# A Fourier mixing stage ahead of two expert layers: two bias products side by side on row halves

## Chip, cores and metric

The kernel runs on one core of a Trainium2 chip. The metric is the device time of one execution in microseconds (us), as a median of several runs.

## The reference

```python
def _attn_ref(x, w_r, w_i, b_r, b_i):            # x: 2 x 3008 x 256
    X = np.fft.rfft(x, axis=1)
    Xr, Xi = X.real, X.imag
    Yr = Xr @ w_r - Xi @ w_i + b_r
    Yi = Xr @ w_i + Xi @ w_r + b_i
    Yr = np.sign(Yr) * np.maximum(np.abs(Yr) - 0.01, 0.0)
    Yi = np.sign(Yi) * np.maximum(np.abs(Yi) - 0.01, 0.0)
    return np.fft.irfft(Yr + 1j * Yi, n=3008, axis=1)

h = x @ moe_w_in                                  # 6016 tokens, 256 -> 2048
x = (h * np.clip(h + 3.0, 0.0, 6.0) / 6.0) @ moe_w_out
g = x @ moe2_w_gate                               # 256 -> 1536
out = (g / (1 + np.exp(-g)) * (x @ moe2_w_val)) @ moe2_w_out
```

## The kernel before

All of it is one program on one core, its order written out by hand: each engine gets its instructions in the order in which the Python code issues them. The first stage, to about 160 us, is the Fourier mixing; the two expert layers fill the rest.

**The start.** `prepare` issues the loads of the first batch of x on SyncE's queue (SP), with the mixing weights `lin` among them, then the first table `load_m(0, 0)`; GpSimd loads the bias (`b_st`, 64 rows). Sixteen steps `halves1(i)` (L317) do the first transform; each ends in a copy out of PSUM, on ScalarE for even i and on VectorE for odd i (L321). `amid` hangs small jobs behind some of these copies: at 7 GpSimd makes the sum and the difference of the two weight tables (`mixed`, L279); `shifts` adds the threshold to the bias on VectorE (L290), copies it to float32r on ScalarE (L291) and subtracts for the low part on VectorE (L136); `hi` copies a weight table to float32r on ScalarE (L282) and `lo` subtracts for its low part on VectorE (L136). `s2` (L363) needs all sixteen copies.

**The quads.** There are 12 quads p = 0 to 11 (`ORDER`, two batches of six). For each, `s2` does the second transform (64 rows high, two row halves), `ln(p, h)` for h = 0, 1 the mixing, and `ia` (L443, 64 rows high, two row halves) the first inverse. `ln` takes a PSUM tile p3 of one bank, puts the bias into it with one product of 128 rows and 512 columns (L418: `ones`, which holds ones in rows 0 and 32, times `shift`), adds 12 full-height products of 256 columns (L413 to L415), takes a second bank p4 for six more, copies that out (`k1`, L424, ScalarE) and adds it to p3 on VectorE (`yb`, L426), which ends the use of p3. A usual quad runs ln(p, 0), s2(p + 1), ia(p - 1), ln(p, 1). Around quads 3 and 4 the eight steps `quarters1` (L333, 64x64 products on two banks each) of the second batch lie between; quad 4 begins ln(4, 0), `quarters1(3)`, ia(3), `quarters1(4)`. From quad 8 on (`FROM`), `post` (L556, 48 rows high) and `unit` (full height) lie between.

The eight PSUM banks are handed out in a fixed turn by `any_bank`:

```python
turn[0] = (turn[0] + 1) % 8
return (acc_bank if turn[0] in (2, 5, 7) else bank)(shape, name)
```

With each `ln` one step of the weight conversion (`conv1.step`) is queued on ScalarE and VectorE.

Of the kernel before, what the change touches and what calls it, by code (L numbers as in the profile page):

```python
# [14 lines left out]
ALU = mybir.AluOpType  # L15
# [5 lines left out]
SEQ, DIM, NB = 3008, 256, 2  # L21
N1, NG, NJ, K2 = 47, 24, 32, 64
GC = 2 * NG
NQ = NG // 4
LAM = 0.01
# [56 lines left out]
def fourier_moe_kernel(ctx: ExitStack, tc: tile.TileContext, x, lin, bias, w1, w2, fwd1, inv2, fwd2,  # L82
                       inv1, out):
    nc = tc.nc
# [33 lines left out]
    psf = [any_bank]  # L118
    few = [False]

    def woven(t):

        return t.rearrange("p (a b) -> p b a", a=2)

    def pairwise(t):

        return t.rearrange("p (b a) -> p b a", a=2)
# [7 lines left out]
    def low(o, full, hi):  # L135
        nc.vector.tensor_tensor(out=o, in0=full, in1=hi.bitcast(F32), op=ALU.subtract)  # L136
# [87 lines left out]
    zeros = xs_p.tile([128, 512], F32, tag="r", name="zeros", bufs=3)  # L224
# [4 lines left out]
    shift = ap_.tile([128, 2 * DIM], F32R, name="shift")  # L229
    ones = ap_.tile([128, 128], F32R, name="ones")  # L230
# [5 lines left out]
    def ring4(name):  # L236
        return ap_.tile([128, 4 * DIM], F32, tag="bc", name=name, bufs=2)
# [4 lines left out]
    def load_x(b, k, c=slice(0, RC), every=((0, 1),)):  # L242
        for p, step in every:
            nc.sync.dma_start(room[b, k][p::step, c], x[b, k, p::step, c])
# [9 lines left out]
    p = psf[0]([128, 512], "p0")  # L254
# [4 lines left out]
    def prepare():  # L259
        lin_st = ring4("lin_st").rearrange("p (k a b) -> p k a b", k=2, a=2)  # L260
        b_st = spread("b_st")
        load_x(0, 1, every=some)
        load_x(0, 2, every=some)
        nc.sync.dma_start(lin_st, lin)
        for c in (slice(0, 2 * TC), slice(2 * TC, RC)):
            load_x(0, 3, c, some)
        load_m(0, 0)
        nc.gpsimd.dma_start(b_st[:64], bias)
        o = spread("o_st")[:, :128]
        nc.gpsimd.memset(o, 0.0)  # L270
        for r in (0, 32):
            nc.gpsimd.memset(o[r : r + 1], 1.0)
        nc.gpsimd.tensor_copy(ones, o)
        nc.gpsimd.tensor_copy(shift[64:], zeros[64:])
        w = [lin_st[:, k] for k in range(2)]

        def mixed(op):
            w.append(spread("mixed").rearrange("p (a b) -> p a b", b=DIM))
            nc.gpsimd.tensor_tensor(out=w[-1], in0=w[1], in1=w[0], op=op)  # L279

        def hi(i, k):
            nc.scalar.copy(linh[:, i], w[k])  # L282

        def lo(i, k):
            low(linl[:, i], w[k], linh[:, i])

        def shifts(i):
            b = b_st[:64]
            if i == 0:
                nc.vector.tensor_scalar(b, b, LAM, None, op0=ALU.add)  # L290
                nc.scalar.copy(shift[:64], b)  # L291
            else:
                low(shift[32:64], b[32:], shift[32:64])

        amid.update({
            7: [lambda: mixed(ALU.subtract), lambda: mixed(ALU.add)], 8: [lambda: shifts(0)], 9: [lambda: shifts(1)],
            12: [lambda: hi(2, 0)], 13: [lambda: lo(2, 0)], 14: [lambda: hi(0, 2), lambda: lo(0, 2)],
            15: [lambda: hi(1, 3), lambda: lo(1, 3)]})

    amid = {}  # L300

    def spread(name):
        return xs_p.tile([128, 2 * DIM], F32, tag="r", name=name, bufs=3)
# [41 lines left out]
    def table(tag, src, Q, n, name):  # L345
        t = ap_.tile([128, n, 128], F32, tag=tag, name=name, bufs=2)
        nc.sync.dma_start(t, src[:, Q * n * 128 : (Q + 1) * n * 128].rearrange("r (g c) -> r g c", g=n))
        return t

    def load_m(b, Q):  # L350
        if (b, Q) not in m_t:
            m_t[b, Q] = table("m", fwd2, Q, 8, f"m{b}_{Q}")
# [34 lines left out]
    def flush():  # L387
        while due:
            due.pop(0)()
# [8 lines left out]
    def ln(b, Q, h):  # L398

        if (b, Q) not in n_t:  # L400
            n_t[b, Q] = table("n", inv1, Q, 4, f"n{b}_{Q}")
        if ORDER.index((b, Q)) <= FROM:
            conv1.step()
        flush()
        xs = [t[:, :, :, h * 128 : (h + 1) * 128] for t in X[b, Q]]

        def product(o, form, k, start):
            o = pairwise(o)
            for dh in range(2):
                xh, xl = (t[:, dh, form] for t in xs)  # L410
                wh, wl = linh[:, k, dh], linl[:, k, dh]
                wh, wl = woven(wh), woven(wl)
                nc.tensor.matmul(o, xh, wl, start=start and dh == 0, stop=False, skip_group_check=not start)  # L413
                nc.tensor.matmul(o, xh, wh, start=False, stop=False, skip_group_check=not start)
                nc.tensor.matmul(o, xl, wh, start=False, stop=dh == 1, skip_group_check=not start)  # L415

        p = psf[0]([128, 2, DIM], f"p3_{b}_{Q}_{h}")
        nc.tensor.matmul(pairwise(p.rearrange("r c d -> r (c d)")), ones, woven(shift), start=True, stop=True)  # L418
        product(p[:, 1], 0, 0, False)
        product(p[:, 0], 1, 1, False)  # L420
        p1 = psf[0]([128, DIM], f"p4_{b}_{Q}_{h}")
        product(p1, 2, 2, True)
        k1 = ap_.tile([128, DIM], F32, tag="k1", name=f"k1{b}_{Q}_{h}", bufs=2)
        nc.scalar.copy(k1, p1)  # L424
        yb = xs_p.tile([128, 2, DIM], F32, tag="r", name=f"yb{b}_{Q}_{h}", bufs=3)
        nc.vector.tensor_tensor(out=yb, in0=p, in1=k1.unsqueeze(1).to_broadcast([128, 2, DIM]), op=ALU.add)  # L426
        yc = xs_p.tile([128, 2, DIM], F32, tag="r", name=f"yc{b}_{Q}_{h}", bufs=3)
        y = yp[b, Q, h] = ap_.tile([128, 2, DIM], F32, tag="yp", name=f"yp{b}_{Q}_{h}", bufs=3)

        def then():  # L430
            nc.scalar.activation(yc, yb, AF.Relu, bias=edges)
            nc.vector.scalar_tensor_tensor(out=y, in0=yb, scalar=0.0, in1=yc, op0=ALU.min, op1=ALU.add)

        later.append(then)

    def ia(b, Q):
        c4 = ring4(f"cs{b}_{Q}")
        p = [psf[0]([128, 2, DIM], f"p5_{b}_{Q}_{i}") for i in range(2)]
        for h in range(2):
            for c in range(2):  # L440
                for i in range(2):
                    r = slice(64 * i, 64 * i + 64)
                    nc.tensor.matmul(p[i][:, h], n_t[b, Q][r, 2 * h + c, :], yp[b, Q, h][r, c, :], start=c == 0,  # L443
                                     stop=c == 1, tile_position=(64 * i, 0))
        for i in range(2):
            nc.scalar.copy(c4.rearrange("r (h i d) -> r i h d", i=2, d=DIM)[:, i], p[i])
        nc.gpsimd.dma_start(Cd[b][:, Q * 4 * DIM : (Q + 1) * 4 * DIM], c4)
# [4 lines left out]
    ORDER = [(b, Q) for b in range(NB) for Q in range(NQ)]  # L452
    FROM = 8
# [8 lines left out]
    def L(p):  # L462
        return [lambda h=h: ln(*ORDER[p], h) for h in range(2)]

    def A(p):
        return [lambda: ia(*ORDER[p])] if p >= 0 else []
# [159 lines left out]
    at = [0]  # L626
# [130 lines left out]
    halves = [(z - a) // 2 for a, z in pairs]  # L757
# [404 lines left out]
    for q in range(len(quads2) + 1):  # L1162
        if q < len(quads2) and quads2[q][1] == 0 and quads2[q][0] + 1 < len(pairs):
            p = quads2[q][0] + 1
# [63 lines left out]
```

## Time and profile before

| | us |
|---|---|
| median of 3 runs | 1129.22 |
| lowest, highest | 1127.73, 1958.57 |
| profiled execution | 1128.69 |
| its span on the core | 1126.9 |

The profile is of one execution; it shows, for each engine, its instructions with start and length, what they waited for, and the chain of waits that ended last. A line such as L418 is a line of the kernel. "PE" is TensorE's products, "PEld" its weight loads, DVE VectorE, ACT ScalarE, POOL GpSimd, SP SyncE with its DMA queue. Lengths of products are modelled; the distance between starts is the safer measure.

### The profile page before, as it was taken

The numbers are of one execution on the slowest core, as the hardware profiler recorded it, in microseconds if no ns is written. First come the engines' busy times: TensorE is split into PE (matmuls) and PEld (weight loads), VectorE is DVE, ScalarE is ACT, GpSimd is POOL, SyncE is SP. The second block draws the span as 40 slices with busy tenths as digits, with TensorE's granted clock in tenths as the row PEclk, the third lists the DMA queues.
The fourth block names the chain that finished last, engine by engine and source line by source line (L and its number), as shares of the span: only waits on it lengthen the run. The fifth ranks groups of instructions, "written<-read, shape, count | busy, mean of one in ns | idle before, by whom it ended". The sixth has DMA issues, their size and how long they took to land.

```text
span 1126.9 us, 19804 instructions
## 1 busy us (share of the span) xinstructions
PE 1115.0 (99%) x7468; PEld 989.5 (88%) x7468; DVE 909.5 (81%) x1635; ACT 775.8 (69%) x1440; POOL 43.0 (4%) x68
## 2 busy tenths in 40 slices
PE   8999999999999999999999999999999999999998
PEld 7999888888888888888899888888888888888997
DVE  5888887999999999999988777777777777777765
ACT  4767676788787787877777666666666656666655
POOL 3000006300000000000000000000000000000000
PEclk9999999999999999999999999999999999999999
DMA  7756335864483573644553544644644644644552
GB/s 294 289 189 229 115 118 177 287 220 144 138 278 107 182 254 108 220 172 138 211 202 140 196 165 162 241 161 165 238 163 165 236 168 169 238 168 168 209 207 75
DMA packets 62944, 211.49 MB, mean 188 GB/s; under 512 B 5984, under 2 KB 23552, under 8 KB 51392
## 3 DMA queue, kind: packets, MB, share of 16 engines
q1 hardware_dynamic: 60784, 203.61, 52.1%
q0 software_dynamic: 1776, 6.42, 1.4%
q8 instruction: 59, 0.97, 0.3%
q14 instruction: 37, 0.30, 0.1%
q10 hardware_dynamic: 288, 0.19, 0.1%
HBM read 170.09 MB, written 40.11 MB: 187 GB/s over the span
## 4 chain that ended last, share of the span: by engine, by line
PE 88%; DVE 7%; ACT 2%; issue 1%; DMA 1%; POOL 0%; ACTq 0%; DVEq 0%; SPq 0%; POOLq 0%
PE acc L131 11%; PE acc L133 11%; PE acc L132 11%; PE P L916 8%; PE P L918 8%; PE P L917 8%; PE Tb L918 4%; PE Tb L916 4%; PE Tb L917 4%; PE p L443 2%; PE p L363 2%; PE Q L918 2%; PE Q L917 2%; PE Q L916 2%; DVE r L964 1%; PE p L415 1%
## 5 line engine op out<-in xcount | busy, mean ns | idle before, releaser
L973 ACT COPY hold<-P 128x512 f32<-128x512 f32 (+1 forms) x224 | 128.2, 572 | 58.3 <-PE P L918 56.9
L596 ACT CAST gated<-r 128x512 fp32r<-128x512 f32 (+1 forms) x160 | 98.1, 613 | 64.9 <-DVE r L964 63.4
L136 DVE TENSOR_TENSOR gated<-s,gated 128x512 fp32r<-128x512 f32 (+1 forms) x144 | 97.4, 677 | 49.8 <-ACT gated L1100 49.5
L136 DVE TENSOR_TENSOR gated<-r,gated 128x512 fp32r<-128x512 f32 (+1 forms) x160 | 108.1, 676 | 21.7 <-ACT gated L596 17.0
L131 PE MATMUL acc<-gated,w_o 128*128 128x512 f32 (+1 forms) x320 | 120.4, 376 | 0.0
L133 PE MATMUL acc<-gated,w_o 128*128 128x512 f32 (+1 forms) x320 | 119.6, 374 | 0.0
L132 PE MATMUL acc<-gated,w_o 128*128 128x512 f32 (+1 forms) x320 | 119.6, 374 | 0.0
L968 DVE TENSOR_TENSOR hold<-Q,hold 128x512 f32<-128x512 f32 (+1 forms) x112 | 75.9, 677 | 43.6 <-ACT hold L973 41.3
L133 PE MATMUL acc<-gated,slot 128*128 128x512 f32 (+1 forms) x288 | 108.1, 375 | 0.0
L131 PE MATMUL acc<-gated,slot 128*128 128x512 f32 (+1 forms) x288 | 108.0, 375 | 0.1
L132 PE MATMUL acc<-gated,slot 128*128 128x512 f32 (+1 forms) x288 | 107.9, 375 | 0.0
L968 DVE TENSOR_TENSOR hold<-P,hold 128x512 f32<-128x512 f32 (+1 forms) x112 | 75.8, 677 | 32.5 <-PE P L918 32.5
L1140 ACT ACTIVATE s<-hold 128x512 f32<-128x512 f32 (+1 forms) x72 | 44.9, 623 | 81.3 <-DVE hold L968 81.3
L960 ACT ACTIVATE r<-hold,consts 128x512 f32<-128x512 f32 (+1 forms) x120 | 85.5, 713 | 14.0 <-DVE hold L968 11.9
L916 PE MATMUL P<-xo,slot 128*128 128x512 f32 (+1 forms) x240 | 90.2, 376 | 2.3 <-DVE hold L968 1.2
L1100 ACT CAST gated<-s 128x512 fp32r<-128x512 f32 (+1 forms) x144 | 87.7, 609 | 5.7 <-DVE s L1155 5.5
L918 PE MATMUL P<-xo,slot 128*128 128x512 f32 (+1 forms) x240 | 88.8, 370 | 0.0
L917 PE MATMUL P<-xo,slot 128*128 128x512 f32 (+1 forms) x240 | 88.8, 370 | 0.0
L968 DVE TENSOR_TENSOR hold<-Tb,hold 128x512 f32<-128x512 f32 (+1 forms) x112 | 75.9, 678 | 14.9 <-PE Tb L918 11.2
L964 DVE SCALAR_TENSOR_TENSOR r<-r,hold 128x512 f32<-128x512 f32 (+1 forms) x120 | 81.0, 675 | 2.5 <-ACT r L960 1.5
L1145 ACT ACTIVATE s<-hold 128x512 f32<-128x512 f32 (+1 forms) x72 | 44.8, 623 | 44.2 <-DVE hold L968 44.2
L973 ACT COPY hold<-Tb 128x512 f32<-128x512 f32 (+1 forms) x112 | 65.1, 581 | 3.9
(189 smaller groups left out, 2835.7 us busy)
## 6 DMA issues: line engine op xcount, KB each, us to landing
slot<-Wd SPq DMA_DIRECT2D x72, 1152.0 KB
slot<-Sd SPq DMA_DIRECT2D x40, 896.0 KB
st<-in_w SPq DMA_DIRECT2D x68, 256.0 KB
Wd<-slot SPq DMA_DIRECT2D x12, 1152.0 KB
m<-in_fwd SPq DMA_DIRECT2D x12, 512.0 KB
Cd<-cs POOLq DMA_DIRECT2D x12, 512.0 KB, 5.6
Xd<-x SPq DMA_DIRECT2D x20, 256.0 KB
raw<-Xd SPq DMA_DIRECT2D x5, 1024.0 KB
```

Of the source, the lines that this page charges most:

```text
L131: nc.tensor.matmul(o, wl, xh, start=start, stop=False)
L132: nc.tensor.matmul(o, wh, xh, start=False, stop=False)
L133: nc.tensor.matmul(o, wh, xl, start=False, stop=stop)
L136: nc.vector.tensor_tensor(out=o, in0=full, in1=hi.bitcast(F32), op=ALU.subtract)
L596: nc.scalar.copy(hi[:, :n], g[:, :n])
L916: nc.tensor.matmul(o, wl, hi, start=start, stop=False, skip_group_check=not start)
L917: nc.tensor.matmul(o, wh, lo, start=False, stop=False, skip_group_check=not start)
L918: nc.tensor.matmul(o, wh, hi, start=False, stop=True, skip_group_check=not start)
L964: nc.vector.scalar_tensor_tensor(out=r[:, :n], in0=r[:, :n], scalar=6.0, in1=x[:, :n], op0=ALU.min, op1=ALU.mult)
L968: nc.vector.tensor_tensor(out=h, in0=x[:, :n], in1=c, op=ALU.add)
L973: nc.scalar.copy(c, x[:, :n])
L1100: nc.scalar.copy(hi[:, :nb], t[:, :nb])
```

## The change

The bias comes as 128 equal rows instead of 64, on SP's queue behind the first table instead of GpSimd's; `ones` has ones in rows 0, 32, 64 and 96, and `shift` holds the same bias in both row halves. A bias product now uses one row half, 64 rows high. Behind the inverses of quads 0, 1, 2, 4, 5 and 6 two of them are issued side by side, one on each row half: that of ln(p, 1) and that of ln(p + 1, 0), each into its own p3 bank. The other twelve are issued in `ln` as before, on the upper row half. `shifts` moves from the copies 8 and 9 to 11 and 12, with two subtractions of 32 rows instead of one; two splits `lo` move behind copy 15.

```diff
@@ prepare
-        nc.gpsimd.dma_start(b_st[:64], bias)
+        nc.sync.dma_start(b_st, bias)
...
-        for r in (0, 32):
+        for r in (0, 32, 64, 96):
             nc.gpsimd.memset(o[r : r + 1], 1.0)
         nc.gpsimd.tensor_copy(ones, o)
-        nc.gpsimd.tensor_copy(shift[64:], zeros[64:])
...
         def shifts(i):
-            b = b_st[:64]
             if i == 0:
-                nc.vector.tensor_scalar(b, b, LAM, None, op0=ALU.add)
-                nc.scalar.copy(shift[:64], b)
+                nc.vector.tensor_scalar(b_st, b_st, LAM, None, op0=ALU.add)
+                nc.scalar.copy(shift, b_st)
             else:
-                low(shift[32:64], b[32:], shift[32:64])
+                for r in (slice(32, 64), slice(96, 128)):
+                    low(shift[r], b_st[r], shift[r])
 
         amid.update({
-            7: [lambda: mixed(ALU.subtract), lambda: mixed(ALU.add)], 8: [lambda: shifts(0)], 9: [lambda: shifts(1)],
-            12: [lambda: hi(2, 0)], 13: [lambda: lo(2, 0)], 14: [lambda: hi(0, 2), lambda: lo(0, 2)],
-            15: [lambda: hi(1, 3), lambda: lo(1, 3)]})
+            7: [lambda: mixed(ALU.subtract), lambda: mixed(ALU.add)], 11: [lambda: shifts(0)],
+            12: [lambda: hi(2, 0), lambda: shifts(1)], 13: [lambda: lo(2, 0)],
+            14: [lambda: hi(0, 2), lambda: hi(1, 3)], 15: [lambda: lo(0, 2), lambda: lo(1, 3)]})
@@ ln
-        p = psf[0]([128, 2, DIM], f"p3_{b}_{Q}_{h}")
-        nc.tensor.matmul(pairwise(p.rearrange("r c d -> r (c d)")), ones, woven(shift), start=True, stop=True)
+        at = ORDER.index((b, Q)), h
+        if at not in begun_:
+            shifted([at], slice(0, 64))
+        p = begun_.pop(at)
...
+    begun_ = {}
+
+    def shifted(which, *rows):
+        for at, r in zip(which, rows):
+            p = begun_[at] = psf[0]([128, 2, DIM], "p3_%d_%d" % at)
+            nc.tensor.matmul(pairwise(p.rearrange("r c d -> r (c d)")), ones[r], woven(shift[r]), start=True, stop=True,
+                             tile_position=(r.start, 0))
@@ ia
+        p_ = ORDER.index((b, Q)) + 1
+        if p_ < FROM and p_ != NQ - 2:
+            shifted([(p_, 1), (p_ + 1, 0)], slice(0, 64), slice(64, 128))
@@ kernel
-    bias = np.tile(halves(np.concatenate([b_r, b_i])), (64, 1))
+    bias = np.tile(halves(np.concatenate([b_r, b_i])), (128, 1))
```

## Rows read from the trace of the kernel before

**Rows 1.** The page's first part: busy us (share), xinstructions of each engine.

```profile
PE 1115.0 (99%) x7468; PEld 989.5 (88%) x7468; DVE 909.5 (81%) x1635; ACT 775.8 (69%) x1440; POOL 43.0 (4%) x68
```

**Rows 2.** Waits of TensorE from 23 us on: us in total, times, longest.

```profile
PE P L916 <- DVE hold L968: 1.6, 3, 0.8
PE P L916 <- ACT hold L973: 0.9, 1, 0.9
PE p L363 <- issue: 0.6, 1, 0.6
```

**Rows 3.** The chain of waits in order of time, 0 to 60 us: start, us, what.

```profile
9.12 7.50 PE p L317 x176
...
18.93 2.08 PE p L363 x32
...
40.40 1.73 PE p L443 x16
42.13 0.41 PE p L418
...
44.55 0.22 PE p L418
...
49.84 1.93 PE p L443 x16
```

**Rows 4.** Timeline of all engines, 12 to 19 us: start, us, instruction, [idle before <- releaser].

```profile
12.49 0.41 DVE L290 TENSOR_SCALAR b_st<-b_st 64x512 f32<-64x512 f32 x1
12.68 3.07 POOL L279 TENSOR_TENSOR mixed<-lin_st 128x512 f32<-128x512 f32 x2 [5.98 <-DMA lin_st<-in_lin]
13.05 0.62 ACT L291 CAST shift<-b_st 64x512 fp32r<-64x512 f32 x1
...
13.93 0.68 DVE L136 TENSOR_TENSOR shift<-b_st,shift 32x512 fp32r<-32x512 f32 x1
14.66 0.56 DVE L321 COPY zm<-p 128x384 f32<-128x384 f32 x1
...
16.57 0.69 DVE L136 TENSOR_TENSOR linl<-lin_st,linh 128x512 fp32r<-128x512 f32 x1
...
18.28 0.55 DVE L321 COPY zm<-p 128x384 f32<-128x384 f32 x1
```

**Rows 5.** The page's DMA issues: KB, us from issue to landing.

```profile
b_st<-in_bias POOLq DMA_DIRECT2D x1, 128.0 KB, 5.8
```

**Rows 6.** Timeline of SP's queue, 9.5 to 12 us.

```profile
10.72 0.33 SPq L347 DMA_DIRECT2D m<-in_fwd  x1
11.33 0.33 SPq L244 DMA_DIRECT2D second<-in_x  x1
```

**Rows 7.** Waits of SP's queue, 0 to 30 us.

```profile
SPq L347 <- DMA m<-in_fwd: 4.7, 1, 4.7
```

**Rows 8.** Stretches: length, busy (x) PE, PEld, DVE, ACT, POOL, PEclk, DMA share, GB/s.

```profile
4.70:5.60 0.90, 0.90 (x12) 0.90 (x14) 0.00 (x0) 0.00 (x0) 0.81 (x4) 1.00 0.91 328
5.70:6.60 0.90, 0.90 (x26) 0.90 (x24) 0.00 (x0) 0.48 (x1) 0.80 (x2) 1.00 1.05 364
...
17.30:18.90 1.60, 0.00 (x0) 0.00 (x0) 1.23 (x3) 0.85 (x2) 0.00 (x0) 1.00 0.73 302
10.00:16.00 6.00, 6.00 (x152) 6.00 (x149) 3.26 (x7) 3.11 (x7) 3.07 (x2) 1.00 1.01 408
```

**Rows 9.** Timeline of TensorE's weight loads, 2.3 to 3.6 us.

```profile
2.54 0.33 PEld L256 LDWEIGHTS p<-zeros 128*128 128x128 f32 x1 [0.52 <-issue]
3.39 0.33 PEld L256 LDWEIGHTS p<-zeros 128*128 128x128 f32 x1 [0.52 <-issue]
```

**Rows 10.** Timeline of all engines, 58.6 to 61.2 us.

```profile
58.70 1.15 PE L333 MATMUL p<-fwd_sb,second 64*64 64x48 f32 x64
...
59.32 0.42 DVE L199 TENSOR_TENSOR w_c<-wt,w_c 128x256 fp32r<-128x256 f32 x1
...
60.53 0.68 DVE L426 TENSOR_TENSOR yb<-p,k 128x512 f32<-128x512 f32 x1
```

**Rows 11.** Timeline of all engines, 92.5 to 94 us.

```profile
92.63 0.69 DVE L426 TENSOR_TENSOR yb<-p,k 128x512 f32<-128x512 f32 x1
...
93.84 0.48 PE L418 MATMUL p<-shift,ones 128*128 128x512 f32 x1
```

## The prediction

> **What bounds the kernel now.** I began with the page's busy times [rows 1]: TensorE is busy for 1115.0 us, 99% of the span, and no other engine comes near. Then I asked what TensorE waits for after the start [rows 2]: 1.6, 0.9, 0.6 and less, some 3 us in all from 23 us to the end. So behind the start the time is TensorE's own row of products, and a product saved or added there counts in full. The chain of waits in order of time [rows 3] gives the price of a product from the start of one to the start of the next, which the modelled durations don't. A bias product (L418) between two full-height products takes 0.22 us; behind an inverse (L443, 64 rows high) it takes 0.41. The inverse itself takes 1.73 us behind the 64x128 products of L363 and 1.93 behind the 64x64 products of L333. The reader is to see that **a change of tile shape costs 0.19 to 0.20 us** on TensorE, in whichever direction. I take 0.20. In the first 23 us the chain is another: L317's products begin at 9.12, when the x pieces are in, and run to about 17, and then comes a gap until L363 starts at 18.93 [rows 3]. That stage waits for VectorE's copies, so its queue was read next [rows 4].
>
> **The start, first half: when the bias is there.** Before, it went out on GpSimd's queue behind the memsets and landed 5.8 us later [rows 5], ahead of its first use at 12.49 [rows 4]. Now it stands on SP's queue between the two tables. SP issues a transfer only when one that it issued some places earlier has landed, so places in its queue have times of their own: the second table (L347) leaves at 10.72, "second" (L244) at 11.33 [rows 6]. The bias takes the place of 10.72, and the second table that of 11.33. The bias queues behind the first table, which lands at 16.4: the issue of "second" ends at 11.66, and SP then waits 4.7 us for that table [rows 6, 7]. The bias is now 128 rows of 2 KB, 262 KB; at the 408 GB/s of this stretch [rows 8] it needs 0.64 us more, and the 131 KB that GpSimd no longer moves give 0.32 back. **Estimate: it lands at 16.7 us.** The 5.8 us that it took before, counted from 10.72, give 16.5.
>
> **The start, second half: who stands behind it.** Its addition is now queued on VectorE behind copy 11 (14.66 to 15.22) and ahead of copies 13 and 15, and its ScalarE copy ahead of copies 12 and 14. The intervals are those of before [rows 4]: from a landing to a start 0.1 (small beside the rest); addition to ScalarE copy 0.56 (12.49 to 13.05); from that copy's start to the first subtraction's 0.88 (13.05 to 13.93), which holds a wait for copy 9, so that up to 0.2 comes off; then four steps of 0.6 each from start to start (two subtractions of 0.68, copy 13, the split lo(2,0) of 0.69; neighbours overlap by some 0.08); and from copy 15's start to L363's 0.65 (18.28 to 18.93). 16.7 + 0.1 + 0.56 + 0.88 + 4 x 0.6 + 0.65 = 21.3. What the edit removes here, the split lo(0,2) that stood ahead of copy 15, is in the old 18.93 already. **I take 21.1, a loss of 2.2 us.** If the bias landed by 15.2, the same row would give 19.7, a loss of 0.6 (with the 0.2 off); nothing in it gives less, since the shift work now follows copy 11. The upper bound is 2.5, with no bytes given back. The removed zeroing of `shift` and the two added 1-row memsets lie on GpSimd, which idles 5.98 us before the table mixing at 12.68 [rows 4]: they cost nothing, and without that idle time under 0.7. The two splits behind copy 15 end 1.3 us after it, while two runs of L363 of 2 us each [rows 3] stand ahead of the first ln product: hidden; without that cover, 1.3.
>
> **The twelve paired products.** Behind the inverses of quads 0, 1, 2, 4, 5 and 6 two bias products stand on row halves of the shape that the inverse just used, so no change of shape comes in between; the one change that L418 paid now falls on the first L413. Half-height products of different halves run side by side: 16 of L443, 256 columns each, take 1.73 us, 0.108 each [rows 3], while a lone full-height float32 product of 512 columns takes 0.85 at the slower clock (2.54 to 3.39) [rows 9], which is 0.21 for 256 columns at the faster. So a pair costs one slot of 0.22 in place of two: 6 x 0.22 = **1.3 us gained**; nothing if the two ran one behind the other. The two levels show in L317's pace, 12 products in 0.9 us and a little later 26 [rows 8].
>
> **The twelve lone products** keep their length but become 64 rows high. Six follow products that are 64 or 48 high anyway ((0,0), (4,1), (5,0), (8,1), (9,0), (9,1)) and pay one change as before. The other six, (0,1), (1,0), (10,0), (10,1), (11,0) and (11,1), stand between full-height products, where before they cost 0.22 with no change [rows 3]; now each goes in and out: 6 x 2 x 0.20 = **2.4 us lost**. No row shows a single half-height product among full ones: the bounds are 0 and 2.4, and I take the end that every change of shape in the trace shows.
> [...]
>
> **A bank held longer.** The 8 PSUM banks are handed out in turn. With both products of a pair allocated behind the inverse, the bank of p3 of (p+1, 0) is taken several places earlier, and the allocation eight places on gets it sooner after its last reader. I counted the order out. For most it stays harmless: the tightest of the pairs, at 93.84, reuses a bank that VectorE's L426 leaves at 93.32 [rows 11]. One doesn't: p3 of (4, 0) now is followed, eight allocations later, by the second bank of quarters1(3), which runs directly behind ln(4, 0), at 58.70. That bank is free only when VectorE has done L426 of (4, 0), 60.53 + 0.68 = 61.21 [rows 10]. Before, that bank had gone to quarters1(1). VectorE doesn't come to it sooner: from 59.32 to L426 it works off a conversion step queued ahead, without a break [rows 10]. So TensorE stands from 58.7 to 61.3: **2.6 us lost**. The wait of 0.6 that follows [rows 2] hangs on copies behind quarters1(4), and moves along. If my count is off by a place it costs nothing: bounds 0 and 2.8.
>
> **The sum.** The profiled execution took 1128.69 us, 0.5 below the median of 1129.22 and inside the spread. +2.2 + 2.4 + 2.6 - 1.3 = +5.9: **1134.6 us**, 0.5% slower, and so no change that a measurement of this kernel, which tells about 2%, would call one.
>
> **The rivals.**
> (a) *One or two of the charges don't fall due*: the lone products' change is hidden, or the bank is free, or the bias lands by 15.2. Each takes off 1.6 to 2.6, so 1129 to 1133. For it: the lone product and the bank are read from code and pattern, not from a row. Against: [rows 3] know no free change, and SP's queue lands in order.
> (b) *The change does what it is said to do*: the pairs gain 1.3, nothing else is paid, and the start keeps its 18.93: 1127.4, or 1126.5 with earlier x pieces. Against it speaks the landing at 16.7 alone.
> (c) *TensorE's clock falls in the longer gap.* TensorE would stand from about 17 to 21 us, against 1.6 now, after which nothing slowed; the granted clock reads 1.00 there [rows 8], the faster level. [...]
> (d) *The halves of a pair run one behind the other*: the 1.3 isn't gained, 1135.9. L443's pace speaks against it.
> (e) *Slower by over 2%*: the fall of (c), but lasting. At half pace each 1 us of work costs 1 more; past 1151.8 us (1.02 x 1129.2) it gets once 17 us of work behind the start, most of the stretch from 23 to 42 us, run so. Against: at the start the pace rose before the first 6 us were out [rows 8].
>
> **How the numbers follow.** The forecast, all three charges (1133 to 1136.5): 0.50; (a) 0.24; (b) 0.09; (c) 0.11; (d) 0.04; (e) 0.02. The range takes in the forecast, (a), (d) and (c) with the start's upper bound: 1128.5 to 1138.5, about 0.88. Faster by over 2% has no mechanism, 0.01; slower by over 2% is (e), 0.02; within 2% 0.97.
>
> **What would show it.** L363's first start at 21 us with VectorE idle before the bias addition; 12 bias products 0.01 us apart in six pairs, and the next L413 of the following half without a product before it; 0.6 us (not 0.22) for the six lone products between full-height ones; TensorE idle some 2.5 us before or inside quarters1(3), released by L426. It is wrong if the bias lands early, if lone products cost 0.22, or if quarters1(3) starts on time.

## The result, and the profile after

The changed kernel takes **1136.93 us** (median of 6 runs, 1136.36 to 1140.17), the kernel before beside it 1128.74: 8.2 us more. The ratio is 1.0084, 95% interval 1.0072 to 1.0097. One run of the kernel before, of 1958.57 us, stands apart from all others: the median of 1128.74 counts it (without it, 1128.27, and the change costs 8.7 us), the ratio doesn't. The profiled execution took 1136.36 us with a span of 1134.6, 7.7 us over that of before.

The first part of the page of the changed kernel, busy us and share of the span, answers to [rows 1]:

```profile
span 1134.6 us, 19803 instructions
...
PE 1119.0 (99%) x7468; PEld 990.5 (87%) x7468; DVE 910.2 (80%) x1636; ACT 776.4 (68%) x1440; POOL 40.9 (4%) x68
```

TensorE is still the bound, busy for 4 us more with the same number of products. Its waits, in us in total, times and longest, over the whole span (lines have moved: s2 is L362, quarters1 L332, ia L452, the bias product L442, `yb` L427):

```profile
PE p L362 <- ACT linh L281: 3.6, 1, 3.6
PE p L332 <- DVE yb L427: 2.5, 1, 2.5
...
PE P L928 <- DVE hold L980: 1.7, 3, 0.8
```

The first is the stand ahead of s2, the second is new. Before the change the first was:

```profile
PE p L363 <- ACT linh L282: 1.7, 1, 1.7
```

The chain of waits in order of time of the changed kernel (start, us, what) answers to [rows 3]:

```profile
10.80 6.25 DMA b_st<-in_bias
17.07 0.44 DVE b_st L288
17.53 0.62 ACT shift L289
...
21.44 5.43 PE p L362 x63
...
29.33 0.41 PE p L442
29.74 0.31 PE p L412
...
36.55 1.73 PE p L452 x16
38.27 0.21 PE p L442 x2
38.49 0.31 PE p L412
...
65.31 1.14 PE p L332 x62
66.46 3.60 PE p L452 x16
...
74.19 0.41 PE p L442
74.60 0.31 PE p L412
```

Read from the top: the bias's transfer is now on the chain itself. Two runs of s2 take 5.43 us, where before they took some 3.8 (from 18.93 [rows 3] to the first bias product at 22.70). The lone product at 29.33 takes 0.41, and the first L412 behind it 0.31 where 0.11 is usual: 0.61 in place of the 0.22 of [rows 3]. At 38.27 two bias products together take 0.21. The inverse at 66.46 takes 3.60 where it took 1.93 [rows 3].

The timeline of VectorE of the changed kernel at the start, answering to [rows 4]:

```profile
17.07 0.43 DVE L288 TENSOR_SCALAR b_st<-b_st 128x512 f32<-128x512 f32 x1 [1.27 <-DMA b_st<-in_bias]
18.18 1.38 DVE L136 TENSOR_TENSOR shift<-b_st,shift 32x512 fp32r<-32x512 f32 x2 [0.68 <-ACT shift L289]
19.59 0.56 DVE L320 COPY zm<-p 128x384 f32<-128x384 f32 x1
20.18 0.69 DVE L136 TENSOR_TENSOR linl<-lin_st,linh 128x512 fp32r<-128x512 f32 x1
20.79 0.55 DVE L320 COPY zm<-p 128x384 f32<-128x384 f32 x1
```

Copy 13 (19.59) and copy 15 (20.79) stand behind an addition that waits for the bias, though the products that they read were done before 17.9.

TensorE's two slow places show in the granted clock. Stretches of the changed kernel, with columns as in [rows 8]:

```profile
17.70:21.40 3.70, 0.14 (x4) 0.00 (x0) 3.14 (x6) 2.76 (x6) 0.00 (x0) 1.00 0.31 127
22.10:25.40 3.30, 3.30 (x36) 3.30 (x34) 0.44 (x1) 0.69 (x2) 0.00 (x0) 0.50 0.00 0
26.70:66.30 39.60, 37.15 (x575) 33.75 (x572) 32.69 (x79) 27.02 (x69) 1.77 (x3) 1.00 0.80 296
66.50:69.70 3.20, 3.20 (x16) 2.43 (x16) 1.31 (x3) 1.16 (x3) 0.00 (x0) 0.50 0.03 8
```

The granted clock is 0.50 behind each of the two stands: TensorE had been busy for 0.14 of 3.70 us before the first fall, and had waited 2.5 us shortly before the second. In between the granted clock is 1.00, the faster level.

### The profile page after: what moved, and what is told of

The parts are those of the page before. It is cut to its first block, busy times and chain, and to the rows that moved or that the text cites. A ratio compares the mean times of both kernels' runs of the same rounds, so it can differ in the third digit from the quotient of the medians.

```text
span 1134.6 us, 19803 instructions
## 1 busy us (share of the span) xinstructions
PE 1119.0 (99%) x7468; PEld 990.5 (87%) x7468; DVE 910.2 (80%) x1636; ACT 776.4 (68%) x1440; POOL 40.9 (4%) x68
## 4 chain that ended last, share of the span: by engine, by line
PE 92%; DVE 4%; DMA 2%; ACT 1%; issue 1%; POOL 0%; SPq 0%; ACTq 0%; DVEq 0%; POOLq 0%
PE acc L131 12%; PE acc L133 12%; PE acc L132 12%; PE P L928 8%; PE P L930 8%; PE P L929 8%; PE Tb L928 4%; PE Tb L929 4%; PE Tb L930 4%; PE p L362 2%; PE Q L929 2%; PE Q L928 2%; PE Q L930 2%; PE p L452 2%; PE p L412 2%; PE p L568 1%
## 5 line engine op out<-in xcount | busy, mean ns | idle before, releaser
L136 DVE TENSOR_TENSOR gated<-r,gated 128x512 fp32r<-128x512 f32 (+1 forms) x160 | 107.9, 674 | 21.7 <-ACT gated L608 17.2
L928 PE MATMUL P<-xo,slot 128*128 128x512 f32 (+1 forms) x240 | 90.1, 375 | 1.4 <-DVE hold L980 1.2
```

Source lines behind the costliest of these rows:

```text
L928: nc.tensor.matmul(o, wl, hi, start=start, stop=False, skip_group_check=not start)
```

## The experiments

My theory after the result: the 8 us are the three charges of the forecast (late bias, lone products, held bank), and two falls of the clock that the two stands bring. The rivals: the place of the shift work and not the landing; VectorE's backlog and not the bank; a clock that falls for another reason. Ten kernels were run, each beside the kernel before. The ratios are to that one. Gains are counted from the changed kernel's 1136.93, which was measured at another time; beside the kernels the one before took 1128.27 to 1128.68, so that 0.4 us of a gain may be no gain.

**1. The bias early again.**

```diff
-        nc.sync.dma_start(b_st, bias)
+        nc.gpsimd.dma_start(b_st, bias)
```

> The changed kernel with one thing undone: the bias goes out on GpSimd's queue at the start again (now 128 rows), with the jobs behind the copies placed as in the change. Theory (the late landing holds VectorE and ScalarE, and the longer stand lets TensorE's clock fall): the bias is there before copy 11 ends, VectorE's addition starts near 15.3 us, the first product of s2 near 19.5 instead of 21.44, TensorE stands some 2 us and its granted clock does not fall at the start: 1.9 + 1.6 = 3.5 us less, about 1133.4. Rival (the place of the shift work and its second subtraction are the cause, not the landing): s2 starts at 21.4 still, and the time stays at 1136.9. Second rival (the clock falls for another reason than the stand): s2 starts early, but the granted clock still falls near 22 us: 1135.

Measured: 1135.33 us (1134.22 to 1135.92), ratio to before 1.0061 (1.0046 to 1.0076). The s2 products begin at 19.62, TensorE's wait for them is down from 3.6 us (a line of the chain of waits, and one of TensorE's waits):

```profile
19.62 2.08 PE p L362 x32
PE p L362 <- ACT linh L281: 1.5, 1, 1.5
```

and the granted clock stays up there. So the landing is the main cause, and the first rival is out as such. But the time fell by 1.6 us and not by 3.5. Around quarters1(3) the clock is low for longer here than in the changed kernel, whose row stands first:

```profile
58.00:75.00 17.00, 14.55 (x339) 12.57 (x339) 10.16 (x30) 8.88 (x26) 0.53 (x1) 0.90 0.57 191
58.00:75.00 17.00, 14.55 (x278) 12.47 (x280) 8.94 (x26) 8.40 (x23) 0.53 (x1) 0.80 0.54 181
```

From the start of quarters1(3) to the next s2 this takes 1.2 us more (62.27 to 69.30, against 65.31 to 71.13). And the first ln stands 0.4 us behind VectorE again, as before the change; the profile of the changed kernel has no such stand.

**2. The bias late, but nobody behind it.**

```diff
-            7: [...], 11: [lambda: shifts(0)],
-            12: [lambda: hi(2, 0), lambda: shifts(1)], 13: [lambda: lo(2, 0)],
-            14: [...], 15: [lambda: lo(0, 2), lambda: lo(1, 3)]})
+            7: [...], 12: [lambda: hi(2, 0)], 13: [lambda: lo(2, 0)], 14: [...],
+            15: [lambda: shifts(0), lambda: lo(0, 2), lambda: lo(1, 3), lambda: shifts(1)]})
```

> The changed kernel with the bias still on SP's queue, but the shift work placed behind copy 15, so that no copy stands behind the bias: addition, the two splits lo(0,2) and lo(1,3), then the two subtractions. Theory (what counts is who is queued behind the late bias): copy 15 ends near 18.3 us, s2 starts near 18.4, the clock does not fall at the start, and the first ln still finds its shift ready: 3.0 + 1.6 = 4.6 us less, about 1132.3. Rival (the late bias holds the stage wherever it stands): the first ln product comes later than 3.8 us after the start of s2 by 1 us or more, and the gain is under 3 us.

Measured: 1133.14 us (1132.28 to 1134.62), ratio 1.0046 (1.003 to 1.0063). s2 begins at 18.42, and the first ln product 3.95 us later, as usual (again the chain, and TensorE's wait for s2):

```profile
18.42 2.08 PE p L362 x32
PE p L362 <- ACT linh L281: 0.7, 1, 0.7
```

The late bias cost nothing here, where only the first ln waits for it. The gain is 3.8 us of the expected 4.6; in the profile half of the rest is the stand of 0.4 in the first ln, which is back here too.

**3. No pair over quarters1.**

```diff
-        if p_ < FROM and p_ != NQ - 2:
+        if p_ < FROM and p_ not in (NQ - 3, NQ - 2):
```

> The changed kernel without the pair behind the inverse of quad 2, that is, without (3,1) and (4,0) side by side; both are lone again. Theory (the bank of p3 of (4,0) holds quarters1(3), and the stand there lets the clock fall a second time): TensorE no longer waits 2.5 us for L427 there, the granted clock does not fall near 66 us, the old wait of 0.7 behind quarters1(4) is back, and the two lone products cost 0.22 + 2 x 0.2 more: 2.8 + 1.7 - 0.7 - 0.6 = 3.2 us less, about 1133.7. Rival (VectorE's backlog of conversion steps holds quarters1, whichever bank it is): the wait stays, and the time with it. Second rival (the clock falls there anyway): about 1135.4.

Measured: 1132.92 us (1131.93 to 1134.2), ratio 1.0041 (1.0026 to 1.0056). Timeline of TensorE at quads 3 and 4:

```profile
60.87 0.48 PE L442 MATMUL p<-shift,ones 64*128 64x512 f32 x1
...
63.48 1.15 PE L332 MATMUL p<-fwd_sb,second 64*64 64x48 f32 x64
64.56 1.78 PE L452 MATMUL p<-yp,n 64*128 64x256 f32 x14
```

quarters1(3) starts behind ln(4, 0) without a wait, the inverse follows at its usual pace, and the wait for L427 is gone from the list. VectorE has the same conversion steps, so it is the bank. The wait of 0.7 behind quarters1(4), which I expected to come back, did not: the gain is 4.0 instead of 3.2 us.

**4. Lone products full height.**

```diff
+        nc.gpsimd.tensor_copy(ones1, o)            # ones in rows 0 and 32 alone
...
-            shifted([at], slice(0, 64))
+            p = begun_[at] = psf[0]([128, 2, DIM], "p3_%d_%d" % at)
+            nc.tensor.matmul(pairwise(p.rearrange("r c d -> r (c d)")), ones1, woven(shift), start=True, stop=True)
```

> The changed kernel with the lone bias products full height again (a second table of ones with ones in rows 0 and 32 alone), pairs as changed. Theory (each lone half-height product pays a change of shape in and out): the six between full-height products lose 0.4 each, and the three behind 64x64 or 48x64 products 0.2 each, 3.0 us in all, about 1133.9; a bias product between full-height ones takes 0.22 again instead of 0.62. Rival (the 0.2 lie in the product itself, or are hidden elsewhere, since the expert layers win some time back): the time falls by under 1 us.

Measured: 1134.15 us (1132.65 to 1137.14), ratio 1.0055 (1.0036 to 1.0074). The chain of waits (L423 is the lone product, L447 a pair, L416 the first product of ln behind it):

```profile
27.71 0.22 PE p L423
29.93 0.22 PE p L423
...
35.88 0.21 PE p L447 x2
36.09 0.31 PE p L416
```

0.22 in place of 0.41 + 0.31 - 0.11 = 0.61: the change of shape is the price, 0.39 for each of six. The price rests on this chain and not on the time: the median is near the expected 1133.9, but the runs differ by 4.5 us, with mean granted clocks from 0.993 to 0.998. In the profiled run the clock did not fall at the start, though TensorE stood for 3.0 us there:

```profile
20.00:30.00 10.00, 8.82 (x104) 8.46 (x105) 7.50 (x17) 4.99 (x14) 0.00 (x0) 1.00 0.58 201
```

**5. TensorE kept busy while it stands at the start.**

```diff
+        for _ in range(14 if (b, Q) == ORDER[0] else 0):
+            nc.tensor.matmul(p[0][:, 0], fwd1_sb[:, :128], fwd1_sb[:, :128], start=True, stop=True)
```

> The changed kernel with 14 products of no use (128 columns, float32, the first table against itself) put in front of the first s2, into its first bank, which s2 then overwrites. They wait for nothing that s2 waits for, and fill 3.0 us of TensorE's stand of 3.6 us. Theory (the granted clock falls because TensorE stands): s2 still starts at 21.4, the clock no longer falls near 22 us, the two runs of s2 take 3.8 instead of 5.4 us: 1.6 us less, about 1135.3, with the second fall near 66 us as before. Rival (the clock falls for another reason, such as the load of the other engines or a state of the chip): it falls at 22 us all the same, and the time is 1136.9.

Measured: 1135.47 us (1135.09 to 1136.9), ratio 1.0059 (1.0045 to 1.0073). Stretches, columns as above:

```profile
17.10:20.90 3.80, 3.33 (x29) 3.13 (x28) 3.04 (x6) 2.93 (x6) 0.00 (x0) 1.00 0.43 181
22.10:25.40 3.30, 3.30 (x57) 3.07 (x55) 1.45 (x4) 1.92 (x5) 0.00 (x0) 1.00 0.30 65
63.70:70.40 6.70, 6.42 (x110) 5.16 (x114) 1.54 (x4) 1.89 (x5) 0.00 (x0) 0.50 0.12 48
```

The work with a result waits as long as ever, but the granted clock stays at 1.00 behind it, and 57 products (55 of them of s2) instead of 36 fit into the same 3.3 us. The second fall is there in this profile, and lasts longer than in the changed kernel. It is the slowest of the four runs, 1136.9 us. Two others, of 1135.09 and 1135.3 us, have a mean granted clock of 1.000 over the whole run: in them it hardly fell anywhere, though nothing filled that wait.

**6. Kept busy at both places.**

```diff
+        for _ in range(11 if i == 3 else 0):      # quarters1, besides the 14 of the run before
+            nc.tensor.matmul(p[0][:, :128], fwd1_sb[:, :128], fwd1_sb[:, :128], start=True, stop=True)
```

> As the run before, with 11 more such products in front of quarters1(3), where TensorE waits 2.5 us for the bank of p3 of (4,0). Theory: the wait for L427 stays as the place that holds TensorE, but both falls of the clock are gone, 3.3 us less, about 1133.6: what is left over the kernel before, some 5 us, is the row work that I forecast. Rival: the second fall stays; 1135.3.

Measured: 1134.72 us (1133.76 to 1138.36), ratio 1.0061 (1.0041 to 1.0081).

```profile
22.10:25.40 3.30, 3.30 (x58) 3.07 (x55) 1.45 (x4) 1.92 (x5) 0.00 (x0) 1.00 0.26 53
61.20:65.00 3.80, 3.78 (x88) 3.54 (x86) 2.81 (x8) 1.01 (x3) 0.00 (x0) 1.00 0.77 254
65.20:69.70 4.50, 4.50 (x108) 3.98 (x109) 1.94 (x5) 2.77 (x7) 0.53 (x1) 1.00 0.30 87
```

Both falls are gone where TensorE is kept busy: the stand brings them. In time the two fills took 2.2 us off the changed kernel, less than the 3.3 expected. In the profile the spans differ by 2.6: the stand of 0.4 in the first ln is back, and from the end of ln(4, 0) to the inverse it is 0.1 longer. One of the four runs, at 1138.36 with its clock up, I can't explain. What remains over the kernel before with the clock up is 1134.72 - 1128.33 = 6.4 us by the medians, and 1132.0 - 1126.9 = 5.1 by the spans of the two profiles.

**7. The start alone, on the kernel before.**

```diff
-        nc.gpsimd.dma_start(b_st[:64], bias)
+        nc.sync.dma_start(b_st, bias)
...
-            7: [...], 8: [lambda: shifts(0)], 9: [lambda: shifts(1)],
+            7: [...], 11: [lambda: shifts(0)], 12: [lambda: hi(2, 0), lambda: shifts(1)],
...                                              # splits and shifts as in the change, 24 full-height products
```

> The kernel before with the start of the change alone: bias in 128 rows on SP's queue, the shift work behind copies 11 and 12 with two subtractions, the splits behind copy 15; all 24 bias products full height and none paired (their table has ones in rows 0 and 32 alone). Theory (late landing, and the stand lets the clock fall): s2 starts near 21.3, the clock falls near 22 us, 2.4 + 1.6 us, less 0.5 for a wait at the first ln that goes: about 1131.9, and no wait at quarters1(3). Rival (the start costs only its delay of 2.2): 1130.6, with the clock at its faster level throughout.

Measured: 1131.88 us (1131.47 to 1133.31), ratio 1.0029 (1.0017 to 1.0041), 3.2 us over the kernel before. Stretches:

```profile
17.70:21.30 3.60, 0.26 (x7) 0.07 (x2) 2.79 (x5) 2.93 (x6) 0.00 (x0) 0.99 0.35 145
22.10:25.40 3.30, 3.28 (x30) 3.30 (x32) 1.12 (x2) 0.00 (x0) 0.00 (x0) 0.50 0.00 0
```

Stand and fall of the clock come with the start alone, and there is no wait for L427 in this kernel. In this profile, of a run of 1132.74 us, s2 begins at 22.12, later than the 21.3 expected.

**8. The splits alone, on the kernel before.**

```diff
-            ... 14: [lambda: hi(0, 2), lambda: lo(0, 2)],
-            15: [lambda: hi(1, 3), lambda: lo(1, 3)]})
+            ... 14: [lambda: hi(0, 2), lambda: hi(1, 3)], 15: [lambda: lo(0, 2), lambda: lo(1, 3)]})
```

> The kernel before with one part of the change alone: both hi copies behind copy 14, both splits lo(0,2) and lo(1,3) behind copy 15; bias and products as before. Theory (copy 15 stands behind lo(0,2) in the kernel before): copy 15 begins some 0.8 us earlier, s2 starts near 18.1 instead of 18.93, and the splits end before the first ln: 0.8 us less, about 1127.6. Rival (the splits, now later, hold the eviction of the first s2 or the first ln): no gain, 1128.4.

Measured: 1127.63 us (1125.86 to 1129.64), ratio 0.9992 (0.9983 to 1.0). s2 begins a us earlier in the profile than before:

```profile
17.88 2.08 PE p L363 x32
```

In time the gain of 0.7 us just touches none.

**9. All three charges off, and 10. the same with the bias early.** The edits of 2, 3 and 4 together; then that of 1 as well.

> The changed kernel with all three charges taken off: the shift work behind copy 15, no pair behind the inverse of quad 2, lone products full height. What is left of the change are five pairs side by side and the splits behind the last copy. Theory: s2 starts at 18.4 (0.5 earlier than before the change), no wait at quarters1(3), no fall of the clock, five pairs at 0.22: 0.5 + 1.1 = 1.6 us less than the kernel before, about 1126.8. Rival (some cost of the pairs is still unseen, such as the banks that they hold): no faster than the kernel before, 1128.4 or more.

> The version with all three charges taken off, and the bias back on GpSimd's queue at the start. Theory (with the shift work behind copy 15 it no longer matters by which queue the bias comes): the same 1126.8 as with SP's queue, within 0.5. Rival (256 KB more ahead of the x pieces hold the first transform): up to 0.6 slower.

Measured: 1126.78 us (1125.41 to 1127.25) against 1128.33, ratio **0.9979 (0.997 to 0.9987)**; with the bias early 1126.56 (1124.95 to 1129.42) against 1128.68, ratio 0.9984 (0.9974 to 0.9994). Both beat the kernel before and the changed one, and the queue of the bias makes no difference that these runs show. Of the gain of 1.55 us in run 9, run 8 had 0.7 without any pair, so that some 0.9 are left for the five pairs, of which I expected 1.1; no run has the pairs alone. VectorE at the start of the first:

```profile
17.93 0.56 DVE L324 COPY zm<-p 128x384 f32<-128x384 f32 x1 [0.16 <-PE p L320]
18.41 0.42 DVE L292 TENSOR_SCALAR b_st<-b_st 128x512 f32<-128x512 f32 x1
18.74 1.29 DVE L136 TENSOR_TENSOR linl<-mixed,linh 128x512 fp32r<-128x512 f32 x2
20.04 1.39 DVE L136 TENSOR_TENSOR shift<-b_st,shift 32x512 fp32r<-32x512 f32 x2
```

Copy 15 waits 0.16 us for TensorE and for nothing else; the splits and the shift work that the first ln needs are done by 21.5.

## Why the prediction was right, and where it was off

The forecast was 1134.6, the result 1136.93, which is above the 1133 to 1136.5 that I gave the three charges alone. The three charges and the gain of the forecast are all in the trace, near their sizes, and the clock's fall, rival (c), came on top. There were two falls, of 3.3 us together, and smaller terms that I had not seen partly cancel against the rest (below).

- **The late bias: right.** The issue left at 10.80 (10.72 forecast), VectorE's addition began at 17.07 (16.8), s2 at 21.44 (21.1): 2.5 us where I took 2.2. What stood on SP's queue landed in the order of its issue: the weights (5.50) at 12.6 and the first table (9.58) at 16.4, where SP's waits for them of 0.9 and 3.4 us ended, the bias (10.80) at 17.05. Runs 1 and 2 show that it is the landing together with the copies queued behind it. With the bias early, s2 began at 19.62, where my row gave 19.7: the place of the shift work alone costs 0.7. The x pieces came later too in the changed kernel's profile (TensorE waited 1.9 us for them, before 1.1), but that is not the cause: in runs 3, 5 and 6 the first transform ends by 17.2, and s2 begins at 21.29 to 21.38 all the same.
- **The pairs: right.** Two bias products in 0.21 us, 1.3 us over six pairs.
- **The six lone products: right**, 0.39 each against 0.40 (run 4).
- **The other six: off.** I let them pay one change as before. That holds behind 64x128 products: behind the inverse at 107.86 the lone product takes 0.21 and the first L412 0.31. Behind 64x64 or 48x64 ones, (4,1), (5,0) and (9,0), the lone product is a shape of its own, and a change in and a change out are paid: at 74.19, 78.83 and 113.48 the chain has 0.41 and 0.31 again. 0.2 more for each of three, 0.6 us, which my own row of the inverse (1.73 against 1.93 [rows 3]) could have told me.
- **The held bank: right.** The wait for L427 is 2.5 us; measured from the start of one phase to the next, quarters1(3) to the inverse, the kernel loses 2.8. Run 3 shows that it is the bank.
- **"The wait of 0.6 moves along": wrong.** It is not in the waits of the changed kernel, nor in those of runs 3 and 10, while runs 7 to 9 have a wait at that place, of 0.6 to 1.2 us and with different releasers. From quarters1(4) to s2 the changed kernel takes 0.7 us less. What decides whether the wait is there, no run shows.
- **The clock: the term that was mis-sized.** The sum had it at nothing; I gave its fall a chance of 0.11 at one place, since nothing slowed behind a stand of 1.6 us. It fell at two places. Two runs of s2 took 1.6 us longer, the inverse behind quarters1(3) 1.7: 3.3 us in the profiled run. The two levels that I read from the pace of the first products have a granted clock of 1.00 throughout [rows 8], so that those rows don't show them; the changed kernel's rows do, at 1.00 and 0.50. The range's upper end of 1138.5 holds a price of (c) that no run shows; the runs showed falls of 1.6 and 1.7 us. Runs 5 and 6 show the stand as the cause: with TensorE busy through the same wait, the granted clock stays at 1.00. A stand doesn't always bring the fall, as runs 4 and 5 show; what decides that stays open.

The sum as measured: 2.5 + 2.4 + 2.8 - 1.3 = 6.4, and 3.3 for the clock, 0.6 for three shapes, less 0.7 for the wait that went, 0.4 for one at the first ln, and 0.9 for one on ScalarE in the expert layers that the changed kernel doesn't have [rows 2]: 8.3, against 7.7 between the spans and 8.2 between the medians. The trace bears out the last term: at the first product of the expert layers' L916 (now L928) the changed kernel is 8.95 us behind, 219.18 against 228.14, and at 885 us it gets 1.1 back at one place. Why that wait comes and goes is not shown: run 8 has 0.7 of it, run 9 0.4, run 2 0.2, the others none. With the clock held up the sum is 5.0, and 5.4 with the stand at the first ln, which run 6 has; its profile gives 5.1. That its median gives 6.4, like the first four terms, confirms neither.

## What to carry to other kernels

Where one engine sets the time, a wait can cost more than its length: stands of 2.5 us and more took TensorE to a granted clock of 0.50 here, though not every time, and products of no use kept it at 1.00. The transfer moved to later was paid here by all that was queued behind its first use: s2 began at 21.44 instead of 18.93, and at 18.42 with that use behind the last copy, so move the use, not only the transfer. A buffer taken early from a fixed turn made a later step wait 2.5 us for that buffer's reader here, and this is found by writing out the turn; and a product of another tile shape paid 0.2 us on each side here unless its neighbours had the same shape.

## What I had not expected of the hardware

The clock's fall varies. Behind a stand of 3.6 us it fell in the changed kernel, behind one of 3.0 us (run 4) it did not; behind 2.5 us at quarters1(3) it fell in all five profiles that had the wait unfilled, and in two of them stayed low for longer, but two other runs of run 5's kernel list a mean granted clock of 1.000. Runs of the same kernel differ with it: the changed kernel's slowest run, 1140.17 us, has a mean granted clock of 0.994, its fastest, 1136.36, 0.997.
